# A transformer block on one core: q/k/v by the attention's groups, weight loads in halves, filler products in waits, and other stage priorities

## Chip, core and metric

The kernel runs on one core of a Trainium2 chip. The metric is the device time of one launch in microseconds. Each program was also run once under the hardware profiler; the profile's "span" is the time from the first to the last instruction of that execution.

The engines are called as in the profile: PE (TensorE, matrix products; PEld its weight loads), DVE (VectorE), ACT (ScalarE), POOL (GpSimd) and SP (SyncE, which here only issues DMAs).

## The reference

The input x has 2048 tokens of 512 channels. A condition vector c gives six rows of 512 by `silu(c) @ w_mod`: shift, scale and gate for the attention (sa, ca, ga) and for the feed-forward (sb, cb, gb).

```python
h = _layernorm(x) * (1 + ca) + sa
x = x + ga * A(h, wqkv, wo)
h = _layernorm(x) * (1 + cb) + sb
x = x + gb * B(h, w_gate, w_up, w_down)
```

A is attention with 32 heads of 16 channels. Each token sees 8 keys only: itself and the tokens 2, 4, ... 14 before it; positions before the start are masked. B is `(gelu(h @ w_gate) * (h @ w_up)) @ w_down` with 1792 hidden channels. All arrays are bf16.

## The kernel before

**Stages.** Tokens go through the kernel in groups (GROUPS, L219): two of 256 tokens, then three of 512. The stages of a group are:

- `ln1` (L461): norm statistics on DVE (L471), inverse root on POOL (L433), normalized rows xn on DVE (L428).
- `transposed` (L436 to L459): PE transposes xn into the PSUM tile tp, ACT (L456) or DVE (L451) scales and shifts it into hT, channels on partitions.
- `emit_qkv` (L494): per product group of 512 tokens, twelve steps of four products each (L510), every step evicted by ACT (L520) to qT, kT or vT. V is written to a DRAM scratch `scr` (L523), two DMAs per 512 tokens.
- `emit_attention` (L529): vR reads the shifted copies of V back from scr (L542). DVE multiplies q by the shifted k (pq, L566); PE sums over the head's channels (LT, L576). Then come the maximum (L594 to L606), the exponential on ACT (L613), the sum on PE (ss, L625), its reciprocal on DVE (L629), its spread on PE (rB, L637) and the division on DVE (e, L641). DVE multiplies e by vR (pv, L652 or L658), PE folds it (o_ps, L668), the output projection follows (x_ps, L692), and the second norm with its own transposes makes h2T.
- `emit_ffn` (L715): 14 hidden tiles, gate and up products (g_ps and u_ps, L730), gelu (gl, L739) and copy (ub, L742) on ACT, their product on DVE (hht, L743), then per 128 tokens 14 products with WdP (y_ps, L753), the residual on DVE (ot, L761) and the store (L763).

**q/k/v and attention have different groups here.** `at_q` (L767) says which product group of 512 tokens is made ahead of which attention group: the first 512 tokens are normalized and projected at once, and the attention of the first two groups of 256 both use them.

**The modulation.** `mod_cols` (L398 on) makes shift and scale as columns, by products of one column (L405); ACT copies the shift (L412) and adds 1 to the scale (L410). `mod_row` makes the gates as rows; DVE multiplies them into woP (L778) and WdP (L781).

**Order of the work.** Nothing runs in the order in which it is written down. Every piece of work is an operation with an engine, an estimated duration, the tiles that it reads and writes, and a priority. `Plan.order` (L88) places them one after another by a model: among the ready ones it takes the one with the earliest start on its engine, and of equal ones that with the lowest priority number (PRI, L177). A small margin for each engine (MARGIN) shifts the comparison. A DMA counts as startable when the modelled DMA pipe is no more than AHEAD = 3 us full. Tiles of one kind (tag and sequence) are first touched in the order in which they were declared, and each kind has a fixed number of buffers (BUFS, L174). The instructions are then emitted in that order, and each engine and the SP queue take them strictly in order.

**Loads**, by priority (L349 to L372): x(0,2), x(2,4) (rows of 128 tokens, so 256 tokens each), the modulation's first two parts (wm01), wq, wk, wv, x(4,8), wm2, woP, x(8,12), wm3, wm4, x(12,16), Wg, Wu, wm5, WdP.

**Warm products.** 14 products on zeros (L378) run on PE at the start, before any data is there. A helper `keep_warm` exists and is not called.

## Time and profile before

| what | value |
|---|---|
| median of the runs shown | 265.37 us (3 runs, lowest 264.0) |
| the profiled execution's own time | 265.68 us |
| its span, first to last instruction | 264.0 us |
| PE busy | 248.9 us (94%) |
| DVE busy | 164.6 us (62%) |
| ACT busy | 153.5 us (58%) |
| POOL busy | 19.2 us (7%) |
| HBM read, written | 21.4 MB, 4.21 MB |
| mean granted clock of PE | 0.972 |

Shares of busy time are means over the whole span. Where a stage is bound is read from the stretch that it fills: who is idle there, and what ended the wait. PE's busy time holds the time at a low clock too, so the granted clock stands beside it: 1.0 is full speed. In the timeline, a line gives the start, the duration, the engine, the line of the kernel, the operation with its tiles, the count, and in brackets how long the engine had been idle and what released it.

### The profile page before, as it was taken

The page shows a single profiled execution, that of the slowest core. Times are in us where ns is not written, and L with a number is a line of the kernel's source. Part 1 is how long each engine was busy: PE and PEld are TensorE (multiplying, and loading weights), DVE is VectorE, ACT ScalarE, POOL GpSimd, SP SyncE. Part 2 cuts the span into 40 slices and gives each one's busy share as a digit, 9 for nine tenths or more (in the row PEclk, how much of TensorE's full clock was granted, in tenths as well). Part 3 has the DMA queues.
Part 4 walks back from the last instruction along what each step waited for, and adds up shares of the span by engine and source line. Part 5 has one row for each costly group of instructions (what it writes and reads, how often), then busy time and mean ns, then how long its engine had stood idle before and what let it go on. Part 6 is the DMA issues. An engine that isn't in the chain of part 4 may idle for free.

```text
span 264.0 us, 4327 instructions
## 1 busy us (share of the span) xinstructions
PE 248.9 (94%) x1668; PEld 126.3 (48%) x1668; DVE 164.6 (62%) x313; ACT 153.5 (58%) x274; POOL 19.2 (7%) x44
## 2 busy tenths in 40 slices
PE   8599998799999999997798999999999999999994
PEld 2345545354577749742334444534434544444441
DVE  4349973957599627998736999935984512222111
ACT  1246888768685956624578776274676740667400
POOL 7203220010002000000200000100000100000000
PEclk9779999999999999999599999999999999999999
DMA  6999999994064001384000086011000001100011
GB/s 209 350 258 350 399 223 227 295 242 132 2 168 75 0 2 40 74 188 85 20 4 0 3 205 118 0 42 40 0 4 1 0 0 42 40 0 0 2 40 40
DMA packets 24694, 25.88 MB, mean 98 GB/s; under 512 B 1249, under 2 KB 23010, under 8 KB 24674
## 3 DMA queue, kind: packets, MB, share of 16 engines
q1 hardware_dynamic: 24672, 25.61, 36.4%
q8 instruction: 13, 0.21, 0.3%
q14 instruction: 7, 0.06, 0.1%
q10 hardware_dynamic: 2, 0.00, 0.0%
HBM read 21.40 MB, written 4.21 MB: 97 GB/s over the span
## 4 chain that ended last, share of the span: by engine, by line
PE 79%; DMA 10%; DVE 4%; ACT 3%; issue 2%; SPq 1%; DVEq 0%; ACTq 0%
PE g_ps L730 18%; PE y_ps L753 18%; PE u_ps L730 18%; PE qkv_ps L510 11%; DMA WdP<-in_B_w_down_dram 5%; PE x_ps L692 5%; DMA wm<-in_w_mod_dram 3%; PE LT L576 3%; PE o_ps L668 3%; PE tp L444 2%; DMA scr<-vT 2%; DVE WdP L781 2%; ACT hT L456 1%; PE LT L606 1%; PE rB L637 1%
## 5 line engine op out<-in xcount | busy, mean ns | idle before, releaser
L730 PE MATMUL g_ps<-h2T,Wg 128*128 128x512 bf16 (+1 forms) x280 | 58.5, 340 | 1.0 <-ACT gl L739 1.0
L730 PE MATMUL u_ps<-h2T,Wu 128*128 128x512 bf16 (+1 forms) x280 | 57.9, 338 | 0.0
L753 PE MATMUL y_ps<-WdP,hht 128*128 128x512 bf16 x224 | 50.9, 379 | 0.0
L739 ACT ACTIVATE gl<-g_ps 128x512 bf16<-128x512 f32 x56 | 33.6, 600 | 25.0 <-PE g_ps L730 24.7
L743 DVE TENSOR_TENSOR hht<-gl,ub 128x512 bf16<-128x512 bf16 x56 | 23.4, 421 | 30.2 <-ACT ub L742 29.8
L742 ACT CAST ub<-u_ps 128x512 bf16<-128x512 f32 x56 | 32.8, 586 | 15.5 <-PE u_ps L730 14.8
L730 PEld LDWEIGHTS <-Wg 128*128 128x128 bf16 x280 | 26.8, 98 | 23.9 <-issue 4.3
L730 PEld LDWEIGHTS <-Wu 128*128 128x128 bf16 x280 | 27.2, 98 | 22.1 <-issue 2.1
L566 DVE TENSOR_TENSOR pq<-qT,kT 128x2048 bf16<-128x2048 bf16 x32 | 37.8, 1215 | 0.0
L753 PEld LDWEIGHTS <-hht 128*128 128x128 bf16 x224 | 21.2, 98 | 26.4 <-issue 2.5
L652 DVE TENSOR_TENSOR pv<-e,vR 128x2048 bf16<-128x2048 bf16 x24 | 28.7, 1215 | 0.0
L433 POOL TENSOR_TENSOR rstd<-rstd,neghalf 128x2 f32<-128x2 f32 x16 | 14.3, 907 | 187.3 <-DVE rstd L707 84.8
L761 DVE TENSOR_TENSOR ot<-y_ps,x_sg 128x512 bf16<-128x512 f32 x16 | 10.5, 679 | 23.8 <-PE y_ps L753 23.7
L510 PE MATMUL qkv_ps<-hT,wq 128*128 128x512 bf16 x64 | 18.2, 411 | 1.9 <-ACT hT L456 1.7
L456 ACT ACTIVATE h2T<-tp,modT,scl 128x512 bf16<-128x512 bf16 (+1 forms) x20 | 12.7, 698 | 8.5 <-PE tp L444 8.5
L699 ACT ACTIVATE xn<-x_sg 128x512 bf16<-128x512 bf16 x16 | 10.0, 626 | 12.7 <-DVE x_sg L696 12.4
L510 PE MATMUL qkv_ps<-hT,wk 128*128 128x512 bf16 x64 | 16.6, 387 | 0.0
L692 PE MATMUL x_ps<-woP,oT 128*128 128x512 bf16 x64 | 15.1, 379 | 0.0
L510 PE MATMUL qkv_ps<-hT,wv 128*128 128x512 bf16 x64 | 14.8, 380 | 0.0
L444 PE MATMUL tp<-ident,xn 128*128 128x128 bf16 x128 | 10.6, 236 | 3.6 <-DVE xn L428 3.5
L471 DVE BATCH_NORM_STATS2 st<-x_sg 128x6 f32<-128x512 bf16 x16 | 10.0, 680 | 5.5 <-DMA x_sg<-in_A_x_dram 5.5
L520 ACT CAST qT<-qkv_ps 128x512 bf16<-128x512 f32 x16 | 9.5, 591 | 4.9 <-PE qkv_ps L510 4.9
(84 smaller groups left out, 219.9 us busy)
## 6 DMA issues: line engine op xcount, KB each, us to landing
vR<-scr SPq DMA_DIRECT2D x24, 260.0 KB, 5.4
vR<-scr SPq DMA_DIRECT2D x8, 264.0 KB, 8.3
out_dram<-ot SPq DMA_DIRECT2D x16, 128.0 KB, 1.7
Wg<-in_B_w_gate_dram SPq DMA_DIRECT2D x1, 1792.0 KB, 11.6
Wu<-in_B_w_up_dram SPq DMA_DIRECT2D x1, 1792.0 KB, 13.6
WdP<-in_B_w_down_dram SPq DMA_DIRECT2D x1, 1792.0 KB, 13.5
x_sg<-in_A_x_dram SPq DMA_DIRECT2D x3, 512.0 KB, 7.9
scr<-vT SPq DMA_DIRECT2D x6, 256.0 KB, 3.3
```

Of the source, the lines that this page charges most:

```text
L433: gp(0.75, lambda: nc.gpsimd.tensor_tensor(out=rstd[:], in0=rstd[:], in1=neghalf[:, 0:2], op=ALU.pow), r=[rstd, neghalf], w=[rstd], pri=p)
L444: nc.tensor.transpose(tp[:, dd, c4 * P:(c4 + 1) * P], xn[:, i, dt * P:(dt + 1) * P], ident[:])
L456: act(act_us(n, 2), lambda dt=dt, dd=dd, tp=tp: nc.scalar.activation(out=dst[:, dt, 0:n], in_=tp[:, dd, 0:n], func=ACT.Identity, scale=scl ...
L510: nc.tensor.matmul(ps[:], lhsT=wqkv[b][:, dt, j:D:4], rhs=hT[g][:, dt, :], start=(dt == 0), stop=(dt == DT - 1))
L566: dve(1.145, lambda j=j, wg=wg, no=no, t=pq[m]: nc.vector.tensor_tensor(out=t[:], in0=_ap(q[gq][:, j, o0:o0 + n], [[0, no], [1, n]]), in1= ...
L652: dve(1.145, lambda jj=jj, jl=jl, wg=wg, t=pv[m]: nc.vector.tensor_tensor(out=t[:], in0=_ap(e[:, wg, :], [[0, 4], [1, n]]), in1=vR[g][jj][ ...
L692: nc.tensor.matmul(x1_ps[:], lhsT=oT[:, j, c4 * P:(c4 + 1) * P], rhs=woP[:, j, :], start=(j == 0), stop=(j == 3))
L730: nc.tensor.matmul(ps[:, f, :], lhsT=Wt[:, dt, ft * P:(ft + 1) * P], rhs=h2[g][:, dt, 0:n], start=(dt == 0), stop=(dt == DT - 1))
L739: act(act_us(SG), lambda gl=gl, ps=gu[0]: nc.scalar.activation(out=gl[:], in_=flat(ps), func=ACT.Gelu_apprx_tanh), r=[gu[0]], w=[gl], pri= ...
L742: act(act_us(SG), lambda ub=ub, ps=gu[1]: nc.scalar.copy(out=ub[:], in_=flat(ps)), r=[gu[1]], w=[ub], pri=p)
L743: dve(0.339, lambda gl=gl, ub=ub, ht=hh[u // 2], u=u: nc.vector.tensor_tensor(out=ht[:, u % 2, :], in0=gl[:], in1=ub[:], op=ALU.mult), r=[ ...
L753: nc.tensor.matmul(y_ps[:], lhsT=hh[u // 2][:, u % 2, f * n + c4 * P:f * n + (c4 + 1) * P], rhs=WdP[:, ft, :], start=(ft == 0), stop=(ft = ...
```

## The change

- **q/k/v by the attention's groups.** `at_q` is gone: `ln1` and `emit_qkv` run for each of the five groups, so for 256, 256, 512, 512 and 512 tokens. For a group of 256 a step makes two of the four column sets j into one PSUM bank, eight products of 256 columns. For group 0 the first two steps are four operations each, one per slice dt of 128 channels, which read only that slice of hT. The transposes of a 256-group go to one tile with four slices; for group 0 two slices are evicted by ACT and two by DVE. V of a 256-group is one write to scr.
- **Loads.** Wg, Wu and WdP are loaded in two halves each (`load_rows`). x(2,4) stands behind wk; wv stands behind x(4,8); the late loads are ordered by a table of priorities.
- **Fillers.** Where the plan sees PE wait between the moment a PSUM bank is free and the start of the operation that fills it, up to 16 dummy products are put into that bank first (`filler`).
- **Warm products** are 12 at the start, 8 after c's columns and 4 after the modulation's columns.
- **Priorities and the model's figures** (PRI, MARGIN, AHEAD, the DMA model) come from a search.
- **Small edits.** The scale's "+ 1" goes from ACT to DVE; the last 128 tokens' y_ps, residual and store are made in two halves of 256 columns.

The core of the diff:

```diff
+            if o.pad is not None and o.pad not in seen and o.eng in engines:
+                got, bufs = made[o.pad.tag], self.tags[o.pad.tag][1]
+                came = max(engines[o.eng], got[-bufs].free if len(got) >= bufs else 0.0)
+                o.pads = max(0, min(16, int((at - came - self.SPARE) / self.PAD)))
...
             if o.dma:
-                pipe = max(pipe, at + us + 0.3) + o.dma
-                o.end = pipe + 1.3 + o.late
+                begin = max(pipe, at + us + 0.75)
+                if begin > pipe + 0.3:
+                    idle = begin
+                pipe = begin + o.dma
+                o.end = pipe + 0.9 + (self.SKEW if pipe - idle > 1.5 else 0.25) + o.late
...
+                if o.pads:
+                    self.filler(o.pad.t, o.pads)
                 o.fn()
...
-    "ln1": (-960, -30, 60, 150),
-    "qkv": (-60, 30, 50, 130),
-    "att": (0, 100, 200, 300, 400),
-    "ffn": (1000, 1100, 1200, 1300, 1400),
-    "glu": (-200, -100, 0, 100, 200),
-    "mod": (3.5, 3.6, 3.7),
-    "wo": 4.0,
-    "wd": 500,
-    "scr": -1002,
-    "vR": -1001,
+        "ln1": (-1182.1, -692.4, -164.8, 26.4, 234.7),
+        "qkv": (-339.7, -124.3, 33.9, 275.6, 585),
+        "att": (46.2, -140.9, -234.9, 42.8, 155.5),
+        "ffn": (1968.5, 1157, 1259.3, 1724.2, 780.9),
+        "glu": (-733, -852.9, -1158.1, -42.4, 945.9),
+        "mod": (-447.3, 70.3, 28.1),
+        "wo": 1545,
+        "wd": 147.5,
+        "scr": -1714.5,
+        "vR": -2087.6,
+        "warm": (12, 8, 0, 4),
+        "load": {"wv": -983.08, "x1": -996.19, "x2": -996.09, "wm2": -983, "wo": -895.51, "x3": -973.43, "wm3":
+        -876.09, "wm4": -875.06, "x4": -985.24, "Wg": -874.56, "Wu": -876.59, "wm5": -888.19, "Wd": -885.68},
 }
+Plan.MARGIN = {"pe": -0.15, "act": 0.45, "dve": -1.14, "pool": -0.63, "sp": -0.87}
+Plan.AHEAD = 5.18
+Plan.SKEW = 0.7
...
+    def filler(t, n):
+        shape = list(t.shape)
+        out = t[:] if len(shape) == 2 else t[:].rearrange("p a b -> p (a b)")
+        for i in range(n):
+            nc.tensor.matmul(out, lhsT=ident[:], rhs=BC[:].rearrange("p a b -> p (a b)")[:, 0:out.shape[-1]],
+                             start=True, stop=True)
...
+    def load_rows(t, src, p, cuts, late=0.0):
+        n = len(t.shape) and t.shape[1] // cuts
+        for i in range(cuts):
+            dma(1835e3 / cuts, lambda i=i: nc.sync.dma_start(
+                out=t[:, i * n:(i + 1) * n, :],
+                in_=src[i * n * P:(i + 1) * n * P, :].rearrange("(dt p) f -> p dt f", p=P)),
+                w=[(t, k) for k in range(i * n, (i + 1) * n)], pri=p + 0.1 * i, bw=385e3)
...
-    pe(5.2, lambda: warm_mm(14), r=[(early, 0)], w=[wps], pri=-1000)
+    pe(0.43 * PRI["warm"][0], lambda: warm_mm(PRI["warm"][0]), r=[(early, 0)], w=[wps], pri=-1000)
...
+    keep_warm(PRI["warm"][1], [c_ps], -989)
...
     def emit_qkv(g):
-        q[g] = T("qT", [P, 4, SG], BF16, "qT")
-        vs = [T("vT", [P, 2, HALO + SG], BF16, "vT") for _ in range(2)]
+        tok0, n = GROUPS[g]
+        nj = SG // n
+        q[g] = T("qT", [P, 4, n], BF16, "qT")
+        vs = [T("vT", [P, 2 * nj, HALO + n], BF16, "vT") for _ in range(2 // nj)]
+        order = [(b, j) for j in range(0, 4, nj) for b in range(2)] + [(2, j) for j in range(0, 4, nj)]
...
+            if g == 0 and step < 2:
                 for dt in range(DT):
-                    nc.tensor.matmul(ps[:], lhsT=wqkv[b][:, dt, j:D:4], rhs=hT[g][:, dt, :], start=(dt == 0),
-                                     stop=(dt == DT - 1))
-
-            pe(4 * MM, mm, r=[wqkv[b], hT[g]], w=[ps], pri=p)
+                    pe(2 * 0.115, lambda b=b, j=j, ps=ps, dt=dt: mm(b, j, ps, range(nj), (dt,)),
+                       r=[wqkv[b], (hT[g], dt)], w=[ps], pri=p + 0.01 * dt, pad=ps if dt == 0 else None)
+            else:
+                pe(4 * MM if nj == 1 else 0.92, lambda b=b, j=j, ps=ps: mm(b, j, ps, range(nj), range(DT)),
+                   r=[wqkv[b], hT[g]], w=[ps], pri=p, pad=ps)
...
-        gq = at_q[g]
-        if gq is not None:
-            hT[gq] = T("hT", [P, DT, SG], BF16, "hT")
-            ln1(gq, hT[gq], PRI["ln1"][gq])
-            emit_qkv(gq)
+        hT[g] = T("hT", [P, DT, GROUPS[g][1]], BF16, "hT")
+        ln1(g, hT[g], PRI["ln1"][g])
+        if g == 0:
+            keep_warm(PRI["warm"][3], [(mod0, 1)], -969)
+        emit_qkv(g)
```

The operations that may get fillers are the q/k/v steps, both folds (LT and o_ps), the spread of the softmax sum (rB), the output projection (x_ps) and the gate and up products.

More of the change, by code (lines that the diff above doesn't have):

```diff
@@ L93, in order @@
         ready = [o for o in self.ops if not n_pre[o]]
-        engines, pipe, table = {}, 0.0, None
+        engines, pipe, idle, table = {}, 0.0, 0.0, None
         placed, made = [], {t: [] for t in self.tags}
@@ L434, in invsqrt @@
            r=[rstd, neghalf], w=[rstd], pri=p)
+    tp0 = []
     def transposed(xns, n, dst, off, p, seq, tags, split):
-        for dtp in range(2):
-            tp = T(tags[dtp], [P, 2, SG], BF16, "tp", seq)
+        per = 2 if n == SG else 4
+        for dtp in range(DT // per):
+            tp = T(tags[dtp], [P, per, n], BF16, "tp", seq)
+            tp0.append(tp)
             for half, xn in enumerate(xns):
@@ L441, in trans @@
                     for i in range(2):
-                        for dd in range(2):
-                            dt, c4 = 2 * dtp + dd, 2 * half + i
+                        for dd in range(per):
+                            dt, c4 = per * dtp + dd, 2 * half + i
                             nc.tensor.transpose(tp[:, dd, c4 * P:(c4 + 1) * P], xn[:, i, dt * P:(dt + 1) * P],
                                                 ident[:])
-                pe(0.23, trans, r=[xn, ident], w=[(tp, half)], pri=p)
-            for dd in range(2):
-                dt = 2 * dtp + dd
-                if split and dd == 1:
+                pe(0.115 * per, trans, r=[xn, ident], w=[(tp, half)], pri=p)
+            for dd in range(per):
+                dt = per * dtp + dd
+                if split and dd % 2 == 1:
                     dve(0.07 + n * 1.041e-3, lambda dt=dt, dd=dd, tp=tp: nc.vector.tensor_scalar(
@@ L462, in ln1 @@
         xns = []
-        for half in range(2):
-            tok = SG * g + 256 * half
+        tok0, n = GROUPS[g]
+        for half in range(n // 256):
+            tok = tok0 + 256 * half
             st = T("st", [P, 2, 6], F32, "st", "ln1")
@@ L479, in ln1 @@
                 norm(tok + P * i, xn, i, Mean(mv), rstd, p)
[L480 removed]
+        transposed(xns, n, dst, 0, p, "ln1", ("psL",) if g == 0 else ("psF", "psF"), g == 0)
     class Mean(Tl):
@@ L525, in emit_qkv @@
-                r=[t], w=[(scr, (g, i))], pri=PRI["scr"])
+                out=scr[:, nv * i:nv * (i + 1), lo + tok0:HALO + tok0 + n], in_=t[:, :, lo:]),
+                r=[t], w=[(scr, (g, i))], pri=PRI["scr"], bw=300e3)
     h2 = {}
@@ L538, in emit_attention @@
         for i, t in enumerate(vR[g]):
-            js = [i] if njv == 2 else [0, 1]
-            rs = [(scr, (gg, jj)) for gg in ({gq, (tok0 - HALO) // SG} if tok0 else {0}) for jj in js]
+            rs = [(scr, (gg, i if GROUPS[gg][1] == SG else 0)) for gg in range(max(g - 1, 0), g + 1)]
             for r in range(4):
```

137 lines of the change are left out of this document (75 added, 62 removed).

## The prediction

> **What bounds the kernel now.** I read the whole span first, cut into stretches at the points where the engine of the products (PE) starts, stops or changes its clock. The columns are: the stretch, its length, busy time (and instructions) of PE, PE's weight load, DVE, ACT and POOL, then PE's granted clock, the share of the DMA engines, and GB/s.
>
> ```profile
> 0.00:12.97 12.97, 8.79 (x67) 4.26 (x68) 5.64 (x19) 2.53 (x6) 6.41 (x30) 0.90 0.83 280
> 12.97:17.20 4.23, 4.23 (x11) 1.52 (x11) 0.55 (x2) 1.78 (x3) 0.00 (x0) 0.51 1.08 256
> 17.20:41.20 24.00, 23.64 (x194) 13.19 (x193) 20.35 (x52) 17.85 (x32) 5.56 (x6) 1.00 1.04 307
> 41.20:50.20 9.00, 6.59 (x76) 3.69 (x74) 5.84 (x7) 7.96 (x13) 0.00 (x0) 1.00 1.06 256
> 50.20:123.50 73.30, 73.22 (x594) 44.59 (x595) 56.74 (x93) 46.49 (x87) 2.23 (x2) 1.00 0.43 102
> 123.50:127.00 3.50, 0.39 (x3) 0.01 (x1) 3.37 (x11) 1.30 (x4) 1.73 (x2) 0.90 0.17 61
> 127.00:133.80 6.80, 6.80 (x41) 3.18 (x42) 4.52 (x8) 4.34 (x7) 0.29 (x1) 0.55 0.01 2
> 133.80:142.00 8.20, 7.20 (x40) 2.92 (x39) 2.37 (x5) 7.12 (x11) 0.00 (x0) 1.00 0.00 1
> 142.00:259.75 117.75, 117.75 (x654) 52.95 (x652) 64.07 (x119) 64.11 (x115) 3.01 (x4) 1.00 0.12 30
> 259.75:264.00 4.25, 0.29 (x2) 0.00 (x0) 1.18 (x2) 0.00 (x0) 0.00 (x0) 0.86 0.18 62
> ```
>
> PE is the bound, and nearly everything else hides behind it. From its first q product at 12.97 to its last product at 259.75 are 246.78 us. PE idles in these for 0.36 + 2.41 + 0.08 + 3.11 + 1.00 = 6.96. Two stretches run at a low clock: 4.23 at 0.51 loses 2.07, 6.80 at 0.55 loses 3.06. The rest, 246.78 - 6.96 - 2.07 - 3.06 = **234.7 us**, is work at full clock, and the change takes none of it away. So the most it can win is the start (12.97), the 12.1 us of idle and slow time, and the tail (4.25).
>
> Next, the chain of work that ended last shows what fills the start:
>
> ```profile
> 1.80 8.15 DMA wm<-in_w_mod_dram
> 10.00 0.99 PE modT_ps L405 x32
> 10.99 0.46 PE tp L444 x4
> 11.56 0.55 DVE hT L451
> 12.14 0.79 ACT hT L456
> 12.97 12.56 PE qkv_ps L510 x48
> ```
>
> The modulation's weights land at 9.95, 32 one-column products make shift and scale, four transposes of tokens 256 to 511 are still to do, and two evictions of 512 tokens each stand before the first q product.
>
> Last, the timeline at the places where PE or DVE stood (in brackets: idle before, and what ended it):
>
> ```profile
> 39.52 0.69 DVE L641 TENSOR_TENSOR e<-e,rB 128x512 bf16<-128x512 bf16 x1 [0.99 <-PE rB L637]
> 45.10 4.63 DVE L658 TENSOR_TENSOR pv<-e,vR 128x2048 bf16<-128x2048 bf16 x4 [2.66 <-issue]
> 48.65 0.40 PE L668 MATMUL o_ps<-pv,F 128*32 128x256 bf16 x8 [0.73 <-DVE pv L658]
> 97.55 0.96 DVE L629 RECIPROCAL rinv<-ss 128x128 f32<-128x128 f32 x1 [4.79 <-PE ss L625]
> 126.99 2.00 PE L444 MATMUL tp<-ident,xn 128*128 128x128 bf16 x16 [3.11 <-DVE xn L428]
> ```
>
> Group 0's softmax is normalized at 40.2, but its V products begin at 45.1: 4.9 us in which the copies of V (vR) are not there. At 97.55 DVE had waited 4.8 us, because PE did other work before the small sum that DVE needed. At 123.9 PE has nothing left: the feed-forward of the first two groups is done, and the normalized tokens of group 2 come from DVE 3.1 us later. The clock falls there, which costs 3.06 more.
>
> **The change, part by part.** The profiled execution took 265.68, 1.68 more than its span; the median of the runs shown is 265.37, so its sum stands 0.3 above that.
>
> *Start.* Only 256 tokens are normalized, transposed and modulated before the first q product, and x(2,4) leaves the place ahead of the modulation's weights.
>
> ```profile
> 2.31 0.51 SPq L354 DMA_DIRECT2D wq<-in_A_wqkv_dram  x1
> 2.86 0.51 SPq L354 DMA_DIRECT2D wk<-in_A_wqkv_dram  x1
> 3.41 0.80 SPq L354 DMA_DIRECT2D wv<-in_A_wqkv_dram  x1
> 17.19 2.47 DVE L471 BATCH_NORM_STATS2 st<-x_sg 128x6 f32<-128x512 bf16 x4 [3.03 <-DMA x_sg<-in_A_x_dram]
> ```
>
> ```profile
> wq<-in_A_wqkv_dram SPq DMA_DIRECT2D x1, 512.0 KB, 9.1
> wk<-in_A_wqkv_dram SPq DMA_DIRECT2D x1, 512.0 KB, 10.1
> wv<-in_A_wqkv_dram SPq DMA_DIRECT2D x1, 512.0 KB, 11.4
> vR<-scr SPq DMA_DIRECT2D x8, 264.0 KB, 8.3
> ```
>
> Issue plus time to landing: wq at 11.4, wk at 12.96, wv at 14.8, and tokens 512 to 1023 at 17.19. From wq to wv 1024 KB take 3.4 us, so 256 KB less ahead are 0.85: the modulation's weights land at 9.1, wq at 10.55, wk at 12.1. One-column products end at 10.1; the scale now is made on DVE beside the shift on ACT. Two evictions of 256 tokens are on ACT, two on DVE:
>
> ```profile
> L456 ACT ACTIVATE h2T<-tp,modT,scl 128x256 bf16<-128x256 bf16 x8 | 4.2, 576 | 0.0
> ```
>
> ```profile
> 86.88 0.87 PE g_ps L730 x8
> ```
>
> ```profile
> 1.26 5.94 PE L378 MATMUL warm_ps<-early 128*128 128x512 bf16 x14 [1.26 <-DVE neghalf L270]
> ```
>
> I took the start from these: 10.1 + 0.3 for shift and scale + 0.58 for an eviction is 11.0, and since the first q and k steps are issued per slice of 128 channels, the first needs no second eviction. **First product 11.1** (bounds 10.7, when wq lands, and 12.0, if the warm products below are slow): -1.9. Products of 256 columns with their own weight load take 0.87 for eight (the gate's row), as much as four of 512; so twice the loads cost nothing. The hidden bound is 48 loads of a few ns, under 0.3.
>
> *Clock at the start.* Before, 14 warm products end at 7.2, and only one-column products and transposes follow until 12.97; the stretch from there ran at 0.51. Now 12 warm ones come first, 8 after c's columns and 4 after the modulation's columns, where PE would wait anyway. They cover most of the hole. Between none of the 2.07 left and all of it I take a third, 0.7, since the warm products themselves ran slow (14 in 5.94 us are 0.42 each) and nothing shows where the clock rises.
> The Trainium skill (TensorE: Matmul & The Clock Gate, Part 1: The HAM clock gate) says that the clock rises after a busy window of about 3.4 us that runs free, and falls after an idle one. By that rule 12 slow products and 8 more reach over a whole window, nothing of the 2.07 would be left, and the sum would be 0.7 lower; the row of 14 slow products neither bears this out nor denies it.
>
> *Order of the first loads.* x(0,2), the modulation, wq, wk and x(2,4) are the same five transfers as the first five before, in another order: x(2,4) lands where wk did, at 12.96. Of the same seven, wv is now last, so **wv lands at 17.2** instead of 14.8, and x(4,8) at 14.8. (x(12,16) has a priority ahead of wv, but the plan takes tiles of one kind in order, so it stays behind x(8,12).) PE does q and k of group 0 in four steps of 0.87, from 11.1, with 0.1 lost on wk: done at 14.7. Then v waits for 17.2. Group 1's tokens land at 12.96. The two rows
>
> ```profile
> 3.69 2.47 DVE L471 BATCH_NORM_STATS2 st<-x_sg 128x6 f32<-128x512 bf16 x4 [2.42 <-DMA x_sg<-in_A_x_dram]
> 7.34 1.54 DVE L428 TENSOR_SCALAR xn<-x_sg,mv,rstd 128x512 bf16<-128x512 bf16 x4 [0.70 <-POOL rstd L433]
> ```
>
> give 5.2 from landing to the last of four normalized tiles; for two tiles 2.6 to 5.2, I take 3.6, then 0.4 of transposes and 4 x 0.58 on ACT: 19.3. PE's v products fill 17.2 to 18.9. So new idle of 2.5 + 0.4 = **+2.9** (bounds 0 and 5: wv and the tokens as early as wk before, or DVE busy with group 0's first products ahead of the norm). Before, this stretch had no idle.
>
> *V's way through memory, and halves.* Group 0's v is now one write that needs 256 tokens, not two that need 512, and the weights Wg, Wu and WdP come in pieces of half the size, so vR no longer queues behind 1792 KB of Wu (its 264 KB took 8.3 to land). The three more issues on SP stand ahead of nothing urgent while SP idles. Of the 4.9 us that DVE's V products waited I expect most to go. In itself this gives PE nothing: it moves DVE work ahead. The 2.41 idle in 41 to 50 consists of such waits (two of 0.73) and of waits for evictions; 1.0 stays: **-1.4** (bounds 0 and -2.4).
>
> *Priorities, and the hole at 124.* The order of every engine is new. What has to come earlier is group 2's attention, whose long work is DVE's:
>
> ```profile
> 60.00:70.00 10.00, 9.92 (x87) 5.03 (x86) 6.25 (x14) 7.21 (x14) 0.00 (x0) 1.00 0.27 78
> 90.00:100.00 10.00, 10.00 (x68) 5.49 (x66) 4.10 (x9) 6.20 (x9) 0.00 (x0) 1.00 0.01 3
> 110.00:120.00 10.00, 10.00 (x72) 4.87 (x64) 9.90 (x11) 3.32 (x7) 0.00 (x0) 1.00 0.93 199
> ```
>
> DVE is full just before the hole (9.90 of 10), but idle for 5.9 us in 90 to 100 and 3.8 in 60 to 70. Coming 3.1 us earlier needs a third of that slack, which group 0's earlier V and an earlier sum for the softmax both open. Idle and slow time at 123.5 to 133.8 are 3.11 + 3.06, and the 1.00 until 140.9 is a wait for an eviction: 7.2 in all. I leave 2.0 for what the new order leaves open there or elsewhere: **-5.2** (bounds -7.2, and 0 if the new order has such a hole again).
>
> *Fillers.* PE gets dummy products only where the plan sees a wait of more than 0.45 + 0.22 us between the free bank and the operands. They change no end while the wait is real; they keep the clock up through it. If all the waits that I leave (0.1 + 2.9 + 1.0 + 2.0) were filled and half of them were not real on the chip, 3 us of useless products would stand in their place and no time would be won: they cost nothing against this sum, only the chance to beat it. I count 0.
>
> *Tail.* The last y row comes in two halves of 256 columns:
>
> ```profile
> 259.64 1.29 DVE L761 TENSOR_TENSOR ot<-y_ps,x_sg 128x512 bf16<-128x512 f32 x2 [4.75 <-PE y_ps L753]
> ```
>
> The last addition (half of 1.29, 0.65) becomes about half as long, and the last write half as big: **-0.3** (bounds -0.6 and 0; one write more is issued).
>
> **Sum.** 265.7 - 1.9 (start) - 1.4 (of 2.07: clock at the start) + 2.9 (waits for wv and group 1) - 1.4 (41 to 50) - 5.2 (123 to 142) - 0.3 (tail) = 258.4. By the other way: 11.1 + 234.7 + 3.95 + idle and slow time (0.1 + 0.7 + 2.9 + 1.0 + 2.0 = 6.7) + 1.68 = 258.1. The 0.3 between them are the small idle pieces of before (0.36 + 0.08), which the first keeps, and rounding. I forecast **258.0**, 2.8% below the median.
>
> **The rivals.**
> *The early start is paid back and the hole stays.* The attention of group 2 may be late by the same dependences whatever the order: its projection, norm and transposes follow one another, and DVE is full from 110. Then only 1.5 of the 7.2 go: 258.0 + 3.7 = **261.7**; with 2 more of waiting in the first 20 us, 264. For it speaks the row of 110 to 120; against it the 5.9 idle in 90 to 100. That the change doesn't do what it says belongs here: if the plan sees no waits where the chip has them, no filler stands there, and a clock lost again costs about 3.
>
> *All waits go.* If the plan fills the early waits with group 2's work or the loads land earlier, 11.1 + 234.7 + 3.95 + 1.0 + 1.68 = **252.4**. For it: PE was dense from 50.2 to 123.5 and from 142 on even in the old order. Against it: wv's landing.
>
> *Slower: the gate's weights come last.* Wg stands now behind WdP, Wu and the modulation's last parts; the order of before had it first of these.
>
> ```profile
> GB/s 209 350 258 350 399 223 227 295 242 132 2 168 75 0 2 40 74 188 85 20 4 0 3 205 118 0 42 40 0 4 1 0 0 42 40 0 0 2 40 40
> ```
>
> ```profile
> 73.79 0.87 PE g_ps L730 x8
> ```
>
> All loads up to Wg's last half are 12.8 MB, v's copies of groups 0 and 1 another 2.7. A slice is 6.6 us: eight slices moved 15.2 MB, so 15.5 are through at 54, and 18.2, with group 2's copies ahead, at about 65. Until then PE has 192 q/k/v products (12.56 - 2.07 for 48, so 42 us), and with 11.1 and two attentions (some 9) it is at 65 or later, where the old order began with the gate at 73.8. So it starts to cost when Wg lands after about 68, one us each, and makes the kernel slower than before only from 76 on: **268** at 78. Against it speaks that this is 13 us past the late bound.
>
> **How the numbers follow.** Forecast 0.55 (255.5 to 260), hole stays 0.26, all waits go 0.12, slower 0.07. The range 252.0 to 264.5 takes in the first two rivals and leaves out the slower one and a few of the extremes, under 2 in 10. About 2% is what a measurement can tell from no change, 260.1 here. Faster by over 2%: the third case and nine tenths of the first, with a little of the second, 0.66; within 2%: 0.28; slower by over 2%: 0.06.
>
> **What would show it.** First q product at 10.7 to 12 at a clock near 1.0; wv landing near 17 and PE idle or on fillers from 14.7 to 17.2; the V products of group 0 before 40; no hole of PE above 1 us and no slow clock between 115 and 145; after the first q product 234 to 236 us of work other than fillers. The prediction fails if idle and filler time together stay above 9 us, if the clock at the first products is again 0.5, or if PE waits for Wg.

## The result, and the profile after

The changed kernel takes **252.97 us** (median of four runs, 252.46 to 253.12); the kernel before took 264.00 to 265.37 in three runs of the same comparison, and a fourth of its runs, of 427.57, is left out of the ratio. The ratio is 0.956 (95% interval 0.952 to 0.960), so 4.4% faster. The forecast was 258.0. The profiled execution took 253.12 with a span of 251.4; before it was 265.68 with 264.0.

The span after, cut where PE starts, stops or idles (columns as in the prediction's first view):

```profile
0.00:11.16 11.16, 8.84 (x67) 4.21 (x69) 4.73 (x16) 2.23 (x5) 5.62 (x28) 1.00 0.86 286
11.16:15.10 3.94, 3.94 (x40) 3.91 (x40) 3.10 (x10) 2.39 (x5) 0.69 (x1) 1.00 1.10 348
15.10:35.00 19.90, 19.52 (x147) 14.27 (x147) 17.35 (x45) 17.70 (x32) 4.50 (x6) 1.00 1.03 336
35.00:40.00 5.00, 4.10 (x75) 2.37 (x74) 1.00 (x5) 3.42 (x6) 0.00 (x0) 1.00 1.22 197
40.00:60.00 20.00, 19.77 (x174) 10.91 (x177) 18.30 (x32) 15.68 (x30) 0.69 (x1) 1.00 1.11 270
60.00:118.80 58.80, 58.49 (x504) 37.55 (x509) 49.08 (x81) 39.72 (x74) 2.06 (x3) 1.00 0.33 73
118.80:134.00 15.20, 14.89 (x91) 6.38 (x92) 9.23 (x18) 12.44 (x21) 0.00 (x0) 1.00 0.02 9
134.00:247.60 113.60, 112.80 (x628) 51.82 (x637) 62.73 (x116) 61.58 (x109) 2.72 (x4) 1.00 0.13 32
247.60:251.40 3.80, 0.00 (x0) 0.00 (x0) 0.50 (x2) 0.00 (x0) 0.00 (x0) 0.97 0.12 35
```

The granted clock is 1.00 in every row in which PE works. (In the first row that says little: the 12 warm products at its start took 4.79 us, 0.40 each, the 8 behind them 0.24 each.) Behind the first q product the only stretch with idle time worth the name is 35 to 40 (0.90). The view of PE's waits says the same: behind the first row's, which all versions have, the waits with a named cause add up to 2.0 us (one of 0.2 is left out here).

```profile
PE warm_ps L412 <- DVE neghalf L296: 1.3, 1, 1.3
PE qkv_ps L554 <- ACT hT L495: 1.0, 1, 1.0
PE modT_ps L440 <- DMA wm<-in_w_mod_dram: 0.8, 1, 0.8
...
```

So the 12.6 us of span come from these places:

| place | before | after | won |
|---|---|---|---|
| first q product | 12.97 | 11.16 | 1.81 |
| slow clock after it | 2.07 lost | 0 | 2.07 |
| PE idle between 35 and 60 | 2.41 (41 to 50) | 0.90 + 0.23 | 1.28 |
| hole of group 2, idle and slow clock | 7.17 (123.5 to 142) | 0.31 (118.8 to 134) | 6.86 |
| after the last product | 4.25 | 3.80 | 0.45 |
| rest | | | 0.13 |

From 11.16 to 247.60 PE's busy time adds up to 233.5 at full clock; before it was 234.7. The 1.2 between them are no saved work: 27 matmul records are missing after (1713 products against 1740 weight loads), and the short idle times that this leaves in the dense stretches add up to about as much.

**The start.** The timeline of PE, then a row of ACT's:

```profile
7.90 0.61 PE L483 MATMUL tp<-ident,xn 128*128 128x128 bf16 x8
8.35 0.94 PE L440 MATMUL modT_ps<-scT,wm 128*128 128x1 bf16 x32
9.36 0.81 PE L412 MATMUL warm_ps<-early 128*128 128x512 bf16 x3
11.16 1.05 PE L554 MATMUL qkv_ps<-hT,wq 128*128 128x256 bf16 x8 [0.99 <-ACT hT L495]
...
15.12 1.91 PE L554 MATMUL qkv_ps<-hT,wv 128*128 128x256 bf16 x16
```

```profile
10.55 1.02 ACT L495 ACTIVATE hT<-tp,modT,scl 128x256 bf16<-128x256 bf16 x2 [0.86 <-DVE hT L490]
```

The two engines that evict hT don't work side by side: ACT waits 0.86 until DVE's two are done, although it takes other slices. What releases it is a semaphore of DVE, so this is an order that the program keeps between two engines on one PSUM tile; what the chip would do without it is not shown. The one-column products at 8.35 carry no bracket: PE came to them straight from its warm products and the transposes. Nor do the v products at 15.12: they waited for nothing. The table of DMA issues, and the timeline of SP's queue, show that the loads were there in time:

```profile
wm<-in_w_mod_dram SPq DMA_DIRECT2D x1, 1024.0 KB, 5.4
...
wq<-in_A_wqkv_dram SPq DMA_DIRECT2D x1, 512.0 KB, 6.4
...
wv<-in_A_wqkv_dram SPq DMA_DIRECT2D x1, 512.0 KB, 9.2
```

```profile
1.31 0.45 SPq L385 DMA_DIRECT2D wm<-in_w_mod_dram  x1
...
4.33 1.39 SPq L388 DMA_DIRECT2D wv<-in_A_wqkv_dram  x1
```

Issue plus time to landing: the modulation's weights land at 6.7 and wv at 13.5, where the prediction had 9.1 and 17.2.

**Fillers.** There are none. No instruction of the filler's line is in the trace (in the experiments below they show as products of BC and ident). The 72 more weight loads than before are 10 warm products, 48 of q/k/v in 256 columns and 14 of the last y row in halves. The plan saw no wait long enough at the places where it may fill one.

**The middle.** Group 0's V products on DVE, and one row of PE ahead of them:

```profile
45.31 4.63 DVE L712 TENSOR_TENSOR pv<-e,vR 128x2048 bf16<-128x2048 bf16 x4
```

```profile
39.20 0.55 PE L440 MATMUL modT_ps<-scT,wm 128*128 128x1 bf16 x16 [0.85 <-DMA wm<-in_w_mod_dram]
```

They begin at 45.3, before at 45.1: nothing earlier. What changed is the reason. vR is now there (no bracket), and the softmax comes 5 us later instead, with other work of DVE ahead of it. DVE no longer stands, though. The rows of DVE's middle, before and then after:

```profile
40.00:60.00 20.00, 17.59 (x134) 9.48 (x133) 12.78 (x21) 15.41 (x30) 0.69 (x1) 1.00 1.07 253
60.00:100.00 40.00, 39.92 (x349) 24.63 (x348) 28.79 (x50) 28.42 (x51) 1.54 (x1) 1.00 0.25 60
```

```profile
60.00:100.00 40.00, 39.79 (x356) 26.27 (x359) 33.00 (x49) 28.84 (x52) 0.69 (x1) 1.00 0.23 56
```

DVE (third number) does 18.30 + 33.00 = 51.3 us of work between 40 and 100, where it did 41.6. With that, group 2's output projection, which ended near 123 before, is done by 110:

```profile
108.17 1.89 PE L746 MATMUL x_ps<-woP,oT 128*128 128x512 bf16 x8
```

The norm and transposes that PE stood for at 124 now lie beside the feed-forward of groups 0 and 1. That fits the 6.9 us. That it is their cause is argued from these views and from experiments 2 and 7, since no run moves group 2's attention alone.

### The profile page after: what moved, and what is told of

Its sections match the earlier page's. It is cut to its first block, busy times and chain, and to the rows that moved or that the text cites. A ratio compares the mean times of both kernels' runs of the same rounds, so it can differ in the third digit from the quotient of the medians.

```text
span 251.4 us, 4455 instructions
## 1 busy us (share of the span) xinstructions
PE 242.4 (96%) x1713; PEld 131.4 (52%) x1740; DVE 166.0 (66%) x316; ACT 155.2 (62%) x276; POOL 16.3 (6%) x43
## 4 chain that ended last, share of the span: by engine, by line
PE 76%; DMA 8%; DVE 7%; ACT 3%; SPq 2%; issue 1%; POOL 1%; DVEq 0%; ACTq 0%
PE y_ps L810 19%; PE u_ps L784 18%; PE g_ps L784 17%; PE qkv_ps L554 7%; DMA wm<-in_w_mod_dram 5%; PE x_ps L746 5%; PE o_ps L722 3%; DMA x_sg<-in_A_x_dram 3%; PE LT L630 3%; DVE st L511 2%; PE tp L483 2%; DVE WdP L838 1%; POOL rstd L468 1%; DVE rinv L683 1%; ACT e L667 1%
## 5 line engine op out<-in xcount | busy, mean ns | idle before, releaser
L784 PE MATMUL g_ps<-h2T,Wg 128*128 128x512 bf16 (+1 forms) x274 | 56.9, 336 | 0.3 <-issue 0.2
L810 PE MATMUL y_ps<-WdP,hht 128*128 128x512 bf16 (+1 forms) x231 | 50.6, 366 | 0.4
L810 PEld LDWEIGHTS <-hht 128*128 128x128 bf16 x238 | 22.8, 98 | 23.4 <-issue 0.8
L468 POOL TENSOR_TENSOR rstd<-rstd,neghalf 128x2 f32<-128x2 f32 x16 | 11.4, 719 | 185.7 <-DVE rstd L761 164.8
L819 DVE TENSOR_TENSOR ot<-y_ps,x_sg 128x512 bf16<-128x512 f32 (+1 forms) x17 | 11.1, 659 | 16.4 <-PE y_ps L810 16.3
L554 PE MATMUL qkv_ps<-hT,wq 128*128 128x512 bf16 (+1 forms) x77 | 16.4, 336 | 1.1 <-ACT hT L495 1.0
L554 PE MATMUL qkv_ps<-hT,wk 128*128 128x512 bf16 (+1 forms) x79 | 16.4, 336 | 0.2
L753 ACT ACTIVATE xn<-x_sg 128x512 bf16<-128x512 bf16 x16 | 10.1, 632 | 7.7 <-DVE x_sg L750 7.1
L554 PE MATMUL qkv_ps<-hT,wv 128*128 128x512 bf16 (+1 forms) x79 | 14.8, 336 | 0.1
L750 DVE SCALAR_TENSOR_TENSOR x_sg<-x_ps,x_sg 128x512 bf16<-128x512 f32 x16 | 11.0, 689 | 4.2 <-PE x_ps L746 4.2
L495 ACT ACTIVATE hT<-tp,modT,scl 128x512 bf16<-128x512 bf16 (+1 forms) x18 | 11.4, 707 | 1.2 <-DVE hT L490 0.9
## 6 DMA issues: line engine op xcount, KB each, us to landing
vR<-scr SPq DMA_DIRECT2D x8, 264.0 KB, 9.4
scr<-vT SPq DMA_DIRECT2D x7, 256.0 KB, 8.1
```

The lines of the kernel that those rows point to most:

```text
L468: gp(0.75, lambda: nc.gpsimd.tensor_tensor(out=rstd[:], in0=rstd[:], in1=neghalf[:, 0:2], op=ALU.pow), r=[rstd, neghalf], w=[rstd], pri=p)
L495: act(act_us(n, 2), lambda dt=dt, dd=dd, tp=tp: nc.scalar.activation(out=dst[:, dt, 0:n], in_=tp[:, dd, 0:n], func=ACT.Identity, scale=scl ...
L554: nc.tensor.matmul(ps[:, jl, :], lhsT=wqkv[b][:, dt, j + jl:D:4], rhs=hT[g][:, dt, 0:n], start=(dt == 0 and (jl == 0 or not lone)), stop=( ...
L784: nc.tensor.matmul(ps[:, f, :], lhsT=Wt[:, dt, ft * P:(ft + 1) * P], rhs=h2[g][:, dt, 0:n], start=(dt == 0), stop=(dt == DT - 1))
L810: nc.tensor.matmul(y_ps[:], lhsT=hh[u // 2][:, u % 2, f * n + c4 * P:f * n + (c4 + 1) * P], rhs=WdP[:, ft, lo_d:hi_d], start=(ft == 0), st ...
```

## The experiments

Each run is read by its ratio to the kernel before on its own chip (after: 0.956) and by its trace, since that reference moved by up to 3% between runs: medians of 266.3, 266.1 and 266.5 in the three sets, 263.2 to 270.9 in all. The first set asks whether the parts add up one by one (the old groups, the old order, the warm products, the start).

**1. The old groups.** q/k/v are made for 512 tokens at a time as before; the rest is new.

```diff
-        tok0, n = GROUPS[g]
+        tok0, n = SG * g, SG
```

> Everything of the change but the groups: q, k and v are made for 512 tokens at once again, with the new stage priorities, load order, halves, plan figures and warm products. Theory A (the groups bring the start and group 0's V, the order brings the removal of the hole): first q product back near 13 us, no hole over 1 us at 120 to 135, so 1.8 us of the start and little else given back: 255 us. Rival B (only groups and order together remove the hole, because the figures were searched for these groups): a hole or several of 2 us and more, 258 to 262 us.

Measured: 259.35 us, ratio 0.979 (0.970 to 0.987), span 256.1: 4.7 us of span given back, not 1.8 (the profiled execution is the fastest of the four; by the ratios it is about 6). No hole came up at 115 to 140. PE at the start:

```profile
13.49 1.14 PE L483 MATMUL tp<-ident,xn 128*128 128x128 bf16 x8 [2.90 <-DVE xn L463]
14.43 1.91 PE L288 MATMUL qkv_ps<-BC,ident 128*128 128x512 bf16 x4
16.13 2.06 PE L553 MATMUL qkv_ps<-hT,wq 128*128 128x512 bf16 x8
```

With the modulation's weights ahead of x(2,4), the second half of the 512 tokens is late, PE stands 2.9 us, four fillers go ahead of the first q product, and the clock falls to 0.76 between 10 and 16. So the smaller first group is what allows the new order of the loads: the two parts belong together, and their gain is in the start, as theory A had it, but larger than its own row of the table.

**2. The old stage priorities and load order**, with the new groups and model figures.

```diff
-        "ln1": (-1182.1, -692.4, -164.8, 26.4, 234.7),
-        "att": (46.2, -140.9, -234.9, 42.8, 155.5),
...
+    "ln1": (-960, -960, -30, 60, 150),
+    "att": (0, 100, 200, 300, 400),
...
```

> The new groups, halves, warm products and plan figures with the stage priorities and the load order of before. Theory A (the order removes the hole of 7.2 us, the groups bring only the start): the hole stays in some form, 258 to 260 us, first q product near 12 because tokens 256 to 511 stand ahead of the modulation's weights again. Rival B (the groups alone make group 2 early enough): no hole, 253 to 254 us.

Measured: 262.58 us, ratio 0.989 (0.980 to 0.998), span 261.0. Group 2's transposes on PE:

```profile
124.22 0.51 PE L483 MATMUL tp<-ident,xn 128*128 128x128 bf16 x6 [0.63 <-DVE xn L463]
125.58 0.83 PE L483 MATMUL tp<-ident,xn 128*128 128x128 bf16 x8 [0.84 <-DVE xn L463]
```

The waits are back at the old place, 1.96 us idle between 115 and 140 against 3.16 of idle before, but in short pieces (with 0.82 of fillers) and at full clock. The rest went at the start (first q product at 13.87, a clock of 0.72 between 10 and 16) and between 40 and 60 (2.05 idle). Most of the gain depends on the order, and it isn't one hole that gives it.

**3. Without the kept-warm products.** The 8 and the 4 are left out; the order of all else is held.

```diff
-        pe(MM * n, lambda: warm_mm(n), r=[(early, 0)] + after, w=[wps], pri=p)
+        pe(MM * n, lambda: None, r=[(early, 0)] + after, w=[wps], pri=p)
```

> The changed kernel with the 8 + 4 kept warm products taken out, the order of all else held. Theory A (every us at the start counts, since PE is the bound): the first products run at half clock for about 4 us again, 2.07 us lost: 255.0 us. Rival C (up to 39 us the end is set by the chain of loads and norms, and PE has 1 us of waits there that takes up a late start): the clock is low as well, but under 1 us is lost: 253.0 to 254.0 us. Rival D (the clock is up without them): 253.0 us and a clock of 1.0 in 11 to 15.

Measured: 253.65 us, ratio 0.958 (0.950 to 0.965), span 253.2.

```profile
10.00:16.00 6.00, 4.41 (x21) 3.16 (x22) 3.39 (x10) 2.31 (x5) 0.69 (x1) 0.50 1.10 349
```

The clock is 0.50 from 10 to 16, and group 0's q and k end 2.6 us later (transposes after them at 17.31, not 14.67). The span grew by 1.8 only: PE's idle time at 35 to 40 took up 0.9. In this execution a lost microsecond before 40 doesn't cost a whole one. It is the slowest of the four (252.95 to 254.92), and by the ratios the run can't be told from after: the low clock is shown, its price in the median is under what four executions resolve.

**4. Evictions side by side.** Group 0's transposes go to two PSUM tiles, so that ACT and DVE evict at the same time.

```diff
-        per = 2 if n == SG else 4
+        per = 2 if n == SG or split else 4
...
-                if split and dd % 2 == 1:
+                if split and dtp == 1:
```

> The changed kernel with group 0's transposes in two PSUM tiles, one evicted by ACT and one by DVE, so that ACT's first eviction (10.55) no longer stands behind DVE's two (9.72 to 10.45). First q product at 10.3 in place of 11.16. Theory A (every us at the start counts): 252.1 us. Rival C (the chain of loads and norms sets the end up to 39 us): 253.0 us, and PE waits 0.9 us longer before 40.

Measured: 254.41 us, ratio 0.960 (0.951 to 0.970), span 251.4, the same as after.

```profile
7.86 0.94 PE L440 MATMUL modT_ps<-scT,wm 128*128 128x1 bf16 x32
...
9.84 1.05 PE L555 MATMUL qkv_ps<-hT,wq 128*128 128x256 bf16 x8 [0.16 <-ACT hT L496]
```

```profile
39.20 0.55 PE L440 MATMUL modT_ps<-scT,wm 128*128 128x1 bf16 x16 [0.72 <-DMA wm<-in_w_mod_dram]
```

The first q product comes 1.3 us earlier, but only 0.8 of that is the evictions': from the end of the one-column products to it are 1.04 us (8.80 to 9.84), after 1.87 (9.29 to 11.16). The other 0.5 is the 12 warm products, which took 4.30 us in this execution and 4.79 in after's. Nothing is won: at 39.20 PE meets the same transfer at the same time. (Two of the four executions took 255.6 and 256.0; they were not profiled.) The chain of after, up to there, runs over loads, DVE and SP's queue, not over PE:

```profile
2.91 7.59 DMA x_sg<-in_A_x_dram
...
25.54 13.61 DMA wm<-in_w_mod_dram
```

**5 and 6. That transfer earlier.** The loads of the modulation's parts 3 and 4 are issued ahead of Wu; once with the two tiles of 4, once alone.

```diff
+        sp = [o for o in placed if o.dma]
+        for o in sp[22:24]:
+            placed.remove(o)
+            placed.insert(placed.index(sp[20]), o)
```

> The changed kernel with two edits, the order of all else held: group 0's transposes in two PSUM tiles (first q product at 9.84 in the run before, without a gain in the span), and the two loads of 512 KB of modulation weights (wm3, wm4) issued ahead of Wu's two halves in place of behind them, where their products made PE wait 0.85 us until 39.2. Theory C (up to 39 us the end is set by the chain of loads): that wait goes, the earlier start counts from there, 249.5 to 250.5 us by span. Theory A' (each us at the start counts once PE's later waits are gone too) gives the same sign with at most 2.2 us: 249.2. Rival E (another load or DVE takes the place of the wait): span 251.0 to 251.6, with PE idle elsewhere before 60.

> The changed kernel with the second edit alone: wm3 and wm4 issued ahead of Wu. Theory C: PE's 0.9 us of idle in 35 to 40 goes, span 250.5. Rival E: span 251.4, the wait moves to another place before 60.

Measured: 252.87 us, ratio 0.953 (0.949 to 0.958), span 250.8; and 252.75 us, ratio 0.952 (0.947 to 0.958), span 250.9. The idle time at 35 to 40 goes from 0.90 to 0.05 in both, but 40 to 50 now has 0.46 (0.12 after), as rival E had it. What is left, 0.5 us, can't be told from after with these intervals. Nothing measured here clearly beats the changed kernel.

**7. The old hole filled.** The kernel before gets 14 dummy products on PE where it stood at 124; everything else is as before.

```diff
+            def fillers():
+                for _ in range(14):
+                    nc.tensor.matmul(fill[:], lhsT=ident[:], rhs=BC[:].rearrange("p a b -> p (a b)"), start=True,
+                                     stop=True)
```

> The kernel before with 14 dummy products of 512 columns (about 3.0 us) in PE's wait of 3.1 us at 124, ahead of group 2's transposes; no other edit. Theory (the idle wait is what lowers the clock at 127 to 133.8, which costs 3.06 us): the clock stays at 1.0, and the kernel is 2.5 to 3.1 us faster than the kernel before. Rival (the clock falls for another reason, or the wait moves): no difference.

Measured: 264.68 us, ratio 0.997 (0.993 to 1.001), ten runs; span 263.2. First its rows, then the kernel before's.

```profile
127.00:133.80 6.80, 5.78 (x46) 2.51 (x45) 4.77 (x10) 4.80 (x8) 0.82 (x1) 1.00 0.01 2
```

```profile
123.82 0.59 PE L765 MATMUL y_ps<-WdP,hht 128*128 128x512 bf16 x2
124.25 3.19 PE L721 MATMUL fill_ps<-BC,ident 128*128 128x512 bf16 x14
...
130.92 0.40 PE L579 MATMUL LT<-pq,Mph 128*32 128x512 bf16 x4 [0.73 <-DVE pq L569]
131.25 1.04 PE L742 MATMUL g_ps<-h2T,Wg 128*128 128x512 bf16 x4
...
132.98 1.03 PE L742 MATMUL g_ps<-h2T,Wg 128*128 128x512 bf16 x4
```

```profile
123.29 0.59 PE L753 MATMUL y_ps<-WdP,hht 128*128 128x512 bf16 x2
...
130.94 1.89 PE L730 MATMUL g_ps<-h2T,Wg 128*128 128x512 bf16 x4
...
133.74 1.03 PE L730 MATMUL g_ps<-h2T,Wg 128*128 128x512 bf16 x4
```

The clock stays at 1.00 where it was 0.55. This execution reaches the place 0.53 us late (123.82 against 123.29). Counted from there, the gate's first product comes only 0.2 earlier, because PE, now fast, waits for DVE's products (pq) instead of creeping through the same time; its second four products, and what follows them, come 1.3 earlier. So of the 3.06 us that the prediction booked for the slow clock, some 1.3 were a cost of their own in this trace, and the other 1.8 lay over a wait for DVE. The times bear out no more: 0.8 us by the ratio, and the interval reaches from none to some 2. Most of the 7.2 us at this place is not won by the clock.

**8. The old model figures** (margins, look-ahead, DMA model) under the new priorities, so the plan makes another order of them.

```diff
-Plan.MARGIN = {"pe": -0.15, "act": 0.45, "dve": -1.14, "pool": -0.63, "sp": -0.87}
-Plan.AHEAD = 5.18
-Plan.SKEW = 0.7
```

> The changed kernel with the plan figures of before (margins, AHEAD, the DMA's modelled times) and the new priorities, loads, groups and warm products. Theory F (the priorities carry the gain): no hole of PE over 1 us, 252.5 to 254. Rival G (the figures carry it, because they say when data really comes): holes of 2 us and more, 256 to 259 us.

Measured: 260.20 us, ratio 0.981 (0.975 to 0.987), span 259.4.

```profile
40.00:50.00 10.00, 8.38 (x87) 4.83 (x88) 2.37 (x8) 8.42 (x14) 0.00 (x0) 0.84 1.16 281
```

Waits are spread over four places: 2.1 at the first q product, 1.0 at 20 to 30, 1.62 here, 2.2 at 115 to 140. The clock falls to 0.72 between 10 and 16 and to 0.84 here. Set back alone, the figures cost about as much as all stage priorities and the load order (experiment 2, 0.989); the intervals overlap.

**9. x(2,4) ahead of the modulation's weights**, as in the kernel before; the order of all else is held.

```diff
+        x1, wm = sp[4], sp[1]
+        placed.remove(x1)
+        placed.insert(placed.index(wm), x1)
```

> The changed kernel with one load moved, the order of all else held: tokens 128 to 255 of the second rows, x(2,4), issued ahead of the modulation's first weights again, as before. By the prediction's step (256 KB are 0.85 us) the modulation's weights land 0.85 later and the first q product moves from 11.2 to 12.0; with the waits near 39 taking up 0.9, span 251.4 to 252.0. Rival (one early load's landing is only good to some 2 us between executions): the first q product anywhere between 11 and 13.5, span 251.4 to 253.0.

Measured: 256.39 us, ratio 0.965 (0.956 to 0.975), span 255.0: one load of 256 KB, moved by three places, costs 3.6 us of span (2.5 by the ratios), more than either side of the expectation had. Its early stage, and its row of the DMA issues:

```profile
4.00:8.00 4.00, 4.00 (x24) 1.76 (x23) 2.39 (x8) 0.17 (x1) 2.57 (x12) 1.00 0.73 232
```

```profile
wm<-in_w_mod_dram SPq DMA_DIRECT2D x1, 1024.0 KB, 8.0
```

And the same four microseconds of after:

```profile
4.00:8.00 4.00, 4.00 (x21) 1.61 (x19) 2.55 (x8) 0.17 (x1) 2.55 (x12) 1.00 1.06 390
```

The modulation's weights land at 1.8 + 8.0 = 9.8 instead of 6.7, 3.1 us later for bytes that need 0.7 us at 390 GB/s. The DMA engines stand idle for a part of that time (busy share 0.73 against 1.06, 232 GB/s against 390). PE waits 1.58 us for the weights, and the first q product comes at 12.72. The clock falls too, to 0.65 between 10 and 16 and 0.67 from 16 to 20, although the last warm products stand 0.99 us ahead of the first q product, as in after. On 9.0 us of work these clocks lose 3.1: by this working the slow clock, and not the late start, is most of the 3.6.

**10. Whole loads** of Wg, Wu and WdP.

```diff
-    load_rows(Wg, B_w_gate, L["Wg"], 2)
+    load_rows(Wg, B_w_gate, L["Wg"], 1)
...
```

> The changed kernel with Wg, Wu and WdP loaded whole. The plan's order on PE stays the same. Theory (halves do nothing for PE's waits, since Wg and Wu are read whole and nothing urgent stands between the halves): 252.7 to 253.2. Rival (V's way through memory needs the gaps): V products of group 0 later than 45.3, 254 to 256.

Measured: 253.34 us, ratio 0.951 (0.940 to 0.962). Two of five executions took 255.6 and 256.7, the others 252.6 to 253.3. The profiled one is of the former: the modulation's late parts took 13.8 to land (11.0 after), PE idled 1.5 at 35 to 40, and the clock fell:

```profile
40.00:50.00 10.00, 9.67 (x75) 5.40 (x76) 7.38 (x13) 7.35 (x12) 0.00 (x0) 0.83 0.98 297
```

In the median the halves bring nothing that shows; whether they keep such executions away is not settled by five.

**11. The old priorities of the attention alone.**

```diff
-        "att": (46.2, -140.9, -234.9, 42.8, 155.5),
+        "att": (0, 100, 200, 300, 400),
```

> The changed kernel with the priorities of the attention stages alone set back to those of before (0 to 400 in rising order); the plan puts 11 fillers in its waits, about 2.4 us. Theory H (the hole closes because group 2's attention goes ahead of other work on DVE and PE): group 2's projection (x_ps) ends after 112 instead of 110, a hole or fillers of 2 us and more between 115 and 135, 255 to 258 us. Rival (any order with these groups and loads closes it): no hole, 253 to 254.

Measured: 261.84 us, ratio 0.985 (0.977 to 0.993), span 261.1. The expectation had the place wrong: group 2's projection does end late, at 117.8, but nothing stands for it, and 115 to 140 is dense. The loss is at 42 to 50, where group 0's fold follows DVE piece by piece:

```profile
41.99 2.54 PE L288 MATMUL o_ps<-BC,ident 128*128 128x512 bf16 x11
45.78 0.40 PE L722 MATMUL o_ps<-pv,F 128*32 128x256 bf16 x8 [1.25 <-DVE pv L712]
...
49.18 0.62 PE L722 MATMUL o_ps<-pv,F 128*32 128x256 bf16 x8 [0.52 <-DVE pv L712]
```

In the old priorities group 0's attention goes first, and PE is at its fold before DVE is; the new ones put the q/k/v products of tokens 1024 to 1535 in between. Here the plan did put fillers, 11 of them. They cover 2.5 us, but four short waits of 3.2 us in all follow, and the clock falls all the same, to 0.83 between 40 and 60.

**12. wv behind woP.** The four loads of woP go ahead of wv.

```diff
+        for o in sp[11:15]:
+            placed.remove(o)
+            placed.insert(placed.index(sp[6]), o)
```

> The changed kernel with the four loads of woP (128 KB each, 32 partitions) moved ahead of wv, the order of all else held. It asks why wv landed at 13.5 and not at 17.2. Theory W (woP's loads are slow and held up x(4,8) in the kernel before): wv lands at 16.5 or later and the DMA engines move under 300 GB/s in 12 to 18. Rival (only the bytes ahead count, 512 KB at 350 GB/s): wv lands at 15.0.

Measured: 253.54 us (one run), span 251.8.

```profile
16.47 1.94 PE L558 MATMUL qkv_ps<-hT,wv 128*128 128x256 bf16 x16 [1.55 <-ACT hT L499]
```

```profile
35.00:40.00 5.00, 5.00 (x81) 3.03 (x79) 0.86 (x4) 2.91 (x7) 0.00 (x0) 1.00 1.23 199
```

hT had long been there; what came last was wv, issued at 8.30 (4.33 in after) and 8.1 to land: 16.4, 2.9 later than after and close to theory W's 16.5. So the wait of the prediction was made, 1.55 us, and in this one execution the span grew by 0.4 only, because the 0.9 at 35 to 40 went.

## Why the prediction came out as it did

Direction and range were right, and the gain came at the places that the prediction named: the start, the clock, 41 to 50, the hole and the tail. The number was 5 us too high, and each term can be held against the table.

- **Start, -1.9: measured -1.8**, but by luck: two errors cancel. The modulation's columns were done at 9.3, not 10.1. Their weights landed 2.4 us earlier than worked out, and what held the columns then was PE's own row of warm products and transposes, which the sum left out. In other executions with this order the 12 warm products took 4.05 us (experiment 10) to 5.26 (experiment 11), and the first q product came at 10.53 to 11.63 with them. The evictions took 1.9 (9.3 to 11.16), not 0.9: ACT went behind DVE, and experiment 4 took 0.8 of that off.
- **Clock, -1.4: measured -2.07.** The prediction left 0.7 for want of a row that shows where the clock rises. The 8 products behind c's columns took 1.90 us, 0.24 each, so the clock was already full at 6.2, and it stayed up over the one-column products. Experiment 3 shows the clock without them: 0.50 from 10 to 16. The Trainium skill (TensorE: Matmul & The Clock Gate, Part 1: The HAM clock gate) has it that a busy window of some 3.4 us lifts the clock. The trace agrees: after 4.79 us of warm products it was up. Of the 2.07, nothing was left, as the prediction had worked out from that rule.
- **Early waits, +2.9: measured about 0. This is the step that failed.** "Then v waits for 17.2" came from giving each place in the new order the landing time of the same place before. But these times were not a property of the place: with two 256 KB loads at the head, the DMA engines were less busy from 4 to 8 us (0.73 in experiment 9, 0.93 before, 1.06 after), and what came next was late. With the modulation's 1 MB second, wm, wq and wv land at 6.7, 8.2 and 13.5, where the prediction had 9.1, 10.55 and 17.2. Experiment 9 undoes it by that one move: they land at 9.8, 11.3 and 15.8. So the head of the queue accounts for 2.3 of wv's 3.7 us; where the other 1.4 come from stays open. And the size was wrong a second time: a wait of 1.55 us for wv cost 0.4 in experiment 12, because PE had 0.9 of slack at 35 to 40.
- **41 to 50, -1.4: measured -1.3**, for another reason in part. The V products did not come before 40, they came at 45.3 as before. What went is PE's standing for them, since the q/k/v products of tokens 1024 to 1535 now lie there; experiment 11 puts the old order back and has 3.2 us of such waits.
- **Hole, -5.2: measured -6.9.** The reason given (group 2's attention earlier, by DVE's idle time in 60 to 100) is what the trace shows: 9.7 us more DVE work between 40 and 100. The 2.0 left over for new waits didn't come: 0.31 is idle there, and PE's waits elsewhere add up to 2.0 with those of the start. Experiment 7 corrects the splitting of the old hole, idle 3.11 and clock 3.06: keeping the clock up was worth some 1.3 us there by the trace, and 0.8 by the times (the interval takes in none).
- **Tail, -0.3: measured -0.45.** Halves and doubled weight loads: at nothing, and nothing was seen; a step of eight 256-column products takes the 0.87 that was used (12.05 to 12.92 for two steps' starts). **Fillers, 0:** there are none in the changed kernel.

The errors add up: -2.9 (early waits), -0.67 (clock), -1.66 (hole), -0.15 (tail) and -0.13 (rest), against +0.09 (start) and +0.12 (41 to 50), are -5.3, and 258.4 - 5.3 = 253.1 is the time of the profiled execution.

Of the rivals, "all waits go" (252.4) came nearest to the truth. It had a chance of 0.12 because the landing of wv spoke against it, the same wrong step. "The hole stays" fell with the row of 118.8 to 134, and "Wg last" with the waits of PE: the only one of a gate product is 0.2 of its own issue.

**What stays open.** Which part closes the hole. It stays closed without the groups (1) and without the attention's priorities (11); some 2 us of idle time come back there without the priorities and the loads' order together (2) or without the figures (8). Undoing the groups (1), the priorities with the loads' order (2), the figures (8) or the attention's priorities (11) alone costs 4.7 to 9.7 us of span in the profiled executions, 32 together where 12.6 were won, and each opens waits at places of its own. That shows that the gain hangs on the order as a whole; which priority does what was not separated further. That the old 7.2 us were DVE's lateness is shown from one side only: in experiment 2 the transposes wait for DVE at the old place again, and in experiment 7 a PE at full clock waits for it.

## What to carry to other kernels

Before a stage's gain is booked, look whether the chain that ended last runs through that engine there: here 1.3 us less at PE's start was worth nothing and 1.55 us of new wait cost 0.4, because a transfer and DVE's norms set the time at 39. A slow clock beside a wait for another engine is in part the same cost: of 3.06 us booked, some 1.3 came back when the clock stayed up. And a load's landing time isn't to be carried from one issue order to another by its place; when the head of the queue changes, all of it moves.

## What the runs showed of the hardware

- **The head of the load queue goes with the early rate.** In the first 10 us the four kernels that begin with two loads of 256 KB moved 257 (before), 219, 227 and 218 GB/s (experiments 7, 2 and 9); the ten that have the 1 MB load second moved 265 to 278. That load landed at 9.7 to 10.7 in the four and at 6.6 to 8.7 in the ten; the 256 KB more ahead of it need 0.7 us at 390 GB/s. Why isn't shown. The same load in the same place also varied by execution: the modulation's first weights landed at 6.7 in after and at 8.7 in experiment 3.
- **The same warm products took 4.05 to 5.26 us.** That is the range over the executions that begin with these 12. The 8 behind them, where a kernel has them, took 1.90 each time, so what varies is how early the first 12 got fast. In the kernel before, 14 of them took 5.94, 0.42 each.
- **Loads of woP ahead of wv.** In experiment 12, 512 KB in four loads moved wv's landing by 2.9 us, where 512 KB at 348 GB/s are 1.5. Between 12 and 14 the engines moved 225 GB/s, in after 347; wv was also issued 4.0 us later, and which of the two did it isn't separated. It is one execution, and in experiment 3 wv landed at 15.5 without that edit.
- **Fillers didn't hold the clock through the waits behind them.** In experiment 11 eleven of them were followed by waits of 1.25, 0.73, 0.73 and 0.52 us between folds of 0.4 to 0.6, and the clock was 0.50 from 48 to 54.
